# Output weights loaded head by head, border values stored through SyncE: a two-block transformer on one core

## Chip, cores and metric

One Trainium2 chip, one of its cores. The metric is the device time of one execution in microseconds (us); the kernel before takes 3176.66 us (median of three runs, 3176.52 to 3177.76). The engines are TensorE (PE, with its weight loads as PEld), VectorE (DVE), ScalarE (ACT), GpSimd (POOL) and SyncE (SP, which here only issues DMAs).

## The reference

Four blocks, A, B, A, B, each added to its input after a layer norm. A is a recurrent attention over segments of 32 tokens: 8 memory rows and the segment's 32 rows attend to each other in 32 heads of width 192, and the first 8 rows of the result are the memory of the next segment. B is a linear attention. Cut to A and the order of the blocks:

```python
for s in range(n_seg):                       # 64 segments, one after the other
    h = concatenate([mem, x[:, 32*s:32*s+32]])
    q, k, v = h @ Wq, h @ Wk, h @ Wv         # 640 -> 32 heads x 192
    p = softmax(mask(q @ k.T * 192**-0.5))
    o = einsum('bhte,hed->btd', p @ v, Wo)   # 32 x 192 -> 640
    mem = o[:, :8]; outs.append(o[:, 8:])
x = x + A(layernorm(x)); x = x + B(layernorm(x))
x = x + A(layernorm(x)); x = x + B(layernorm(x))
```

## The kernel before

Each A layer has two stages. **The batched stage** (`A_pre`) works out what doesn't depend on the recurrence: for the last 8 tokens of every segment (the border), keys and queries for all 64 segments in eight passes `keys_and_queries(h, r)`. Here h is a half (32 segments) and r a round, a group of 8 heads. One pass is 120 products of 128x256, evicted in turn by DVE and ACT into a staging buffer (`sts`, two of them) and stored to DRAM as `kqb` with one DMA of 1536 KB. Passes go in pairs (two halves of one round). Beside them `first_values(r)` works out border values of the first segments, evicts them into buffers `vts` and stores each to DRAM (`vb`, 97 KB, two blocks of 64 rows of 776 bytes) with `store_values`, through POOL. In layer 0 the same stage also normalises all rows: small steps of that are run one after each eviction, and POOL issues their loads (`ln_x`) and stores (`xn`).

**The chain** (`A_chain`) then runs the 64 segments, each in four rounds, forward in even segments and backward in odd ones. A round projects Q, K and V (20 products of 128x384 each), takes scores (L1191), attends, and multiplies by the output weights (`wo_round`, L1263). POOL loads the border keys and queries (`load_kqb`, L1123) and values (`extra_v`, L1134) and copies them in (L1130) ahead of the scores. Segment s+1 begins with the memory that segment s gives, so a segment that is late makes all that follow late.

**Output weights.** SBUF holds most weights; some stream in again in every segment. A round's output weights are 12 pieces of 640 columns (128 partitions, 164 KB). Rounds 1 and 2 lie whole in `wo_mid`, the first four pieces of rounds 0 and 3 in `wo_own`, and their other eight share `wo_both` and are streamed in turn (`load_both`, L797, four DMAs of two pieces). The matrix in the input has its rows in another order than the kernel's partitions. So layer 0 first copies all four rounds into a DRAM tensor `wo_rows` in the right order (`lay_out_wo`, L816, 32 DMAs of 240 KB), and `load_wo` (L774) takes from there two pieces at a time over all 128 partitions. `early_wo` and `late_wo` are the places of these loads: part in the batched stage, part in segment 0 of the chain. The staging buffers and the buffers of the border values lie where output weights will lie, so those loads wait for the stores out of them.

**What sets the order.** In layer 0's batched stage and in the chains every engine runs in the order of the code. In layer 2's batched stage only SP does, and a scheduler places the others. SP issues its DMAs strictly in order: one that waits holds up all behind it. SP and ACT issue to one set of eight completion counters that the program hands out in turn; a DMA waits until the one eight places earlier has landed. POOL has eight of its own. `load_slot` (L748) refills the slots of streamed Q, K and V weights; in the chain it is tied to the PE step that frees the slot.

**Constants.** `factors` gives four small tables for masks, which POOL builds in `build_A_consts`. They lie in the tensor `under`, where the chain later keeps its output row.

Of the kernel before, what the change touches and what calls it, by code (L numbers as in the profile page):

```python
# [8 lines left out]
P = 128  # L9
BF16 = mybir.dt.bfloat16  # L10
# [8 lines left out]
OWN = 4  # L19
# [4 lines left out]
VH = 194  # L24
# [98 lines left out]
class Kernel:  # L123
# [139 lines left out]
    def kept_tokens(self, k):  # L263
        return (self.later_tokens if k else self.under[:, self.ot_at:self.ot_at + 320]).rearrange("p (b t) -> p b t", b=self.KC)

    def first_rows(self):
        return self.under[:, self.ot_at + 576:self.ot_at + 736]
# [425 lines left out]
    def factors(self):  # L693

        at, out = self.ot_at + 2 * VH + 384, []
        for n in (64, 64, 16, 16):
            out.append(self.under[:, at:at + n])
            at += n
        return out

    def layer_A(self, xn_dram, at_dram, li, x_raw=None):
        nc, tc = self.nc, self.tc
# [9 lines left out]
        wov = self.A_Wo.rearrange("h d m -> (h d) m").rearrange("(q j f) m -> q f j m", j=6, f=32)  # L712
# [50 lines left out]
        early = {(2, 4), (2, 5), (1, 0), (1, 1), (1, 2), (1, 3), (0, 0), (0, 1), (0, 4), (0, 5)}  # L763

        def load_wo(r, part):
            for k in part:
                if r in (0, 3):
                    for i in (2 * k, 2 * k + 1):
                        assert (i < OWN) == (2 * k < OWN)
                    into = wo_own[r][:, 1280 * k:1280 * k + 1280] if 2 * k < OWN else \  # L770
                        wo_both[:, 1280 * k - own:1280 * k + 1280 - own]
                else:
                    into = wo_mid[:, 7680 * (r - 1) + 1280 * k:7680 * (r - 1) + 1280 * k + 1280]
                nc.sync.dma_start(out=into, in_=self.wo_rows[r, :, 1280 * k:1280 * k + 1280])  # L774
# [21 lines left out]
        def load_piece(into, r, c):  # L796
            self.last_load = nc.sync.dma_start(out=into[:, c:c + 1280], in_=self.wo_rows[r, :, own + c:own + c + 1280])  # L797
            return self.last_load
# [10 lines left out]
        if li == 0:  # L809
            self.wo_rows = dram.tile([4, P, 7680], BF16, name="wo_rows")  # L810

        def lay_out_wo(rs):
            for r in rs:
                for h in range(4):
                    for G in range(2):
                        nc.sync.dma_start(out=self.wo_rows[r, 32 * h:32 * h + 32, 3840 * G:3840 * G + 3840]  # L816
                                          .rearrange("f (j m) -> f j m", m=640), in_=wov[8 * r + 4 * G + h])

        def early_wo(first):
            sooner = {(0, 0), (0, 1), (2, 4), (2, 5)}  # L820
            for r in (0, 2, 1):
                load_wo(r, [k for k in range(6) if (r, k) in early and ((r, k) in sooner) == first])

        def late_wo(r, part=range(6)):
            load_wo(r, [k for k in part if (r, k) not in early])
# [10 lines left out]
    def A_pre(self, xn_dram, li, load_matrix, piece, wo_mid, wo_end, lay_out_wo, early_wo, x_raw):  # L836
# [10 lines left out]
        sts = [wo_mid[:, 6144 * i:6144 * i + 192 * SH].rearrange("p (s f) -> p s f", f=192) for i in range(2)]  # L847
        vts = [wo_end[:, 2 * VH * i:2 * VH * i + 2 * VH] for i in range(2 * NR + 1)]
        self.later_tokens = wo_end[:, (4 * NR + 2) * VH:(4 * NR + 2) * VH + 320]
        with ExitStack() as es:  # L850
# [6 lines left out]
            xT = [wo_end[:, 5120 - 1280 * i:6400 - 1280 * i] for i in range(2)]  # L857
            xB = None
            if x_raw is None:
                xB = [[self.view(LATE - 1280 * (i + 1), 1280) for i in range(2)],  # L860
                      [wo_mid[:, 12288 + 640 * i:12288 + 640 * i + 640] for i in range(2)]]
                xT[0] = self.next_xT[:, :]
# [71 lines left out]
            def first_values(r):  # L934
                for k, G in ((0, 0), (0, 1), (1, 0))[0:2 if r else 3]:
                    ps = ps_.tile([P, 512], F32, name="ps_pre", tag="bank")
                    self.tail_values(ps, lambda b: self.kept_tokens(k)[:, b, :], r, G, piece)
                    vt = vts[2 * NR if k else 2 * r + G]
# [3 lines left out]
            nc.vector.memset(wo_end[:, 0:(4 * NR + 2) * VH], 1.0)  # L942
            if x_raw is not None:
                first = [norm_tasks(lambda x, k=k: gather(x, x_raw, 0, k, (nc.sync, nc.scalar)),
                                    lambda xn, k=k: normed.__setitem__((0, k), xn)) for k in range(NT)]
                for step in zip(*first):
                    for f in step:
                        f()
                warm = ps_.tile([P, 512], F32, name="ps_warm", tag="bank")

                def busy(n):
                    for _ in range(n):
                        nc.tensor.matmul(warm[:, :], lhsT=self.ident[:, :], rhs=wo_end[:, 0:512],
                                         start=True, stop=True, skip_group_check=True)

                busy(12)
# [46 lines left out]
            if x_raw is not None:  # L1003
# [22 lines left out]
                keys_and_queries(0, 0)  # L1026
                first_values(0)
                keys_and_queries(1, 0)
                early_wo(False)
            else:  # L1030
# [4 lines left out]
                first_values(0)  # L1035
                self.build_A_consts()
# [6 lines left out]
                early_wo(True)  # L1043
                keys_and_queries(1, 2)
                first_values(2)
                keys_and_queries(0, 3)
                keys_and_queries(1, 3)
                first_values(3)
                load_round(0)
                keys_and_queries(0, 1)  # L1050
                first_values(1)
                keys_and_queries(1, 1)
                early_wo(False)
# [4 lines left out]
    def A_chain(self, xn_dram, at_dram, li, load_slot, piece, late_wo, load_both, wo, low):  # L1058
# [3 lines left out]
        with tc.tile_pool(name=f"A{li}_ch", reuse_waits="tile", bufs=1) as sp, \  # L1062
# [261 lines left out]
            late_wo(0)  # L1324
# [5 lines left out]
            for s in range(NSEG):  # L1330
# [26 lines left out]
                if s == 0:  # L1357
                    late_wo(3, range(OWN // 2))
# [27 lines left out]
                for n in range(L):  # L1386
# [164 lines left out]
```

## Time and profile before

| | |
|---|---|
| median of three runs | 3176.66 us |
| the profiled execution | 3169.9 us |
| its span | 3168.0 us |
| PE busy | 95% of the span |
| DMA, mean over the span | 237 GB/s |
| vb stores through POOL, layer 0 | 9, landing in 6.0 to 11.9 us |
| copies into `wo_rows` | 32 of 240 KB, landing in 8.1 us |
| loads from `wo_rows` | 560 of 320 KB, landing in 4.8 us |

The profile is of one execution. A row of a timeline has the start, the length, the engine, the line, the instruction and its tiles, a count, and in brackets the idle time before it with what ended it. "issue" means that the engine waited for nothing that the profile shows. A row of DMA queues has packets, MB and the share of sixteen DMA engines that they took in the stretch: q1 is SP's queue, q10 ACT's, q0 POOL's.

### The profile page before, as it was taken

The numbers are of one execution on the slowest core, as the hardware profiler recorded it, in microseconds if no ns is written. First come the engines' busy times: TensorE is split into PE (matmuls) and PEld (weight loads), VectorE is DVE, ScalarE is ACT, GpSimd is POOL, SyncE is SP. The second block draws the span as 40 slices with busy tenths as digits, with TensorE's granted clock in tenths as the row PEclk, the third lists the DMA queues.
The fourth block names the chain that finished last, engine by engine and source line by source line (L and its number), as shares of the span: only waits on it lengthen the run. The fifth ranks groups of instructions, "written<-read, shape, count | busy, mean of one in ns | idle before, by whom it ended". The sixth has DMA issues, their size and how long they took to land.

```text
span 3168.0 us, 141538 instructions
## 1 busy us (share of the span) xinstructions
PE 2993.8 (95%) x59586; PEld 1920.6 (61%) x59586; DVE 2184.4 (69%) x5426; ACT 1906.3 (60%) x4536; POOL 1392.8 (44%) x2872
## 2 busy tenths in 40 slices
PE   8789999999999999899999999999999999998999
PEld 7656666666666665555377566666666666665553
DVE  5467777777777777656644677777777777776565
ACT  3356666666666666646433566666666666666453
POOL 3255555555555555430122555555555555554300
PEclk9999999999999999999999999999999999999999
DMA  9977777877877877840268777777877777778300
GB/s 377 340 263 257 261 248 251 265 257 250 272 252 251 267 256 246 288 166 1 103 246 320 257 255 246 263 264 245 264 259 249 255 261 255 246 259 287 130 1 34
DMA packets 338873, 749.67 MB, mean 237 GB/s; under 512 B 68874, under 2 KB 115330, under 8 KB 335166
## 3 DMA queue, kind: packets, MB, share of 16 engines
q1 hardware_dynamic: 267998, 636.89, 58.3%
q0 software_dynamic: 69376, 100.10, 10.9%
q8 instruction: 469, 7.68, 1.0%
q10 hardware_dynamic: 864, 3.64, 0.3%
q14 instruction: 166, 1.36, 0.1%
HBM read 670.77 MB, written 78.01 MB: 236 GB/s over the span
## 4 chain that ended last, share of the span: by engine, by line
PE 76%; DVE 8%; DMA 6%; issue 5%; ACT 3%; POOL 2%; ACTq 0%; DVEq 0%; SPq 0%; POOLq 0%
PE ps_qk_k L1154 13%; PE ps_qk_q L1154 13%; PE ps_v L1154 12%; PE ps_w L1263 11%; PE ps_s L1191 6%; PE ps_pre L985 4%; PE ps_o L1204 3%; PE kv L1506 2%; DVE raws L1453 2%; ACT raws L1234 2%; DVE hT L1455 2%; PE ps_pq L517 2%; PE ps_t L1217 1%; PE ps_wo L466 1%; DVE QK L1377 1%
## 5 line engine op out<-in xcount | busy, mean ns | idle before, releaser
L1154 PEld LDWEIGHTS <-hT 128*32 128x32 bf16 x30720 | 787.1, 96 | 461.0 <-DVE hT L1455 78.7
L1174 DVE STREAM_TRANSPOSE QK<-raws 128x512 bf16<-128x512 bf16 (+1 forms) x1152 | 730.0, 642 | 219.3 <-ACT raws L1169 163.7
L1130 POOL COPY QK<-kqb 64x192 bf16<-64x192 bf16 x1024 | 349.5, 341 | 486.6 <-PE ps_s L1191 254.1
L1154 PE MATMUL ps_qk_q<-arena,hT 128*32 128x384 bf16 x10240 | 511.3, 327 | 41.4 <-DVE hT L1455 25.6
L1154 PE MATMUL ps_qk_k<-arena,hT 128*32 128x384 bf16 x10240 | 510.1, 328 | 3.0 <-ACT E L1273 1.4
L1169 ACT ACTIVATE raws<-ps_qk_k 128x512 bf16<-128x512 f32 (+1 forms) x640 | 313.5, 510 | 254.0 <-PE ps_qk_k L1154 243.5
L1234 ACT ACTIVATE raws<-ps_o,under 128x192 bf16<-128x192 f32 x1024 | 373.8, 420 | 121.9 <-DVE under L1228 102.5
L1154 PE MATMUL ps_v<-arena,hT 128*32 128x384 bf16 x8192 | 428.4, 326 | 4.0 <-issue 3.0
L1169 ACT ACTIVATE raws<-ps_qk_q 128x512 bf16<-128x512 f32 x512 | 305.7, 597 | 166.6 <-PE ps_qk_q L1154 153.1
L1134 POOL DMA_DIRECT2D Vp<-vb x512 | 257.9, 504 | 316.6 <-PE ps_t L1217 210.7
L1123 POOL DMA_DIRECT2D kqb<-kqb x512 | 292.4, 571 | 69.7 <-POOL QK L1130 59.4
L1191 PEld LDWEIGHTS <-QK 128*80 128x80 bf16 x4096 | 196.0, 121 | 184.9 <-issue 153.8
L1183 DVE CAST Vp<-ps_v 64x384 bf16<-64x384 f32 x512 | 286.3, 559 | 24.5 <-ACT Vp L1181 8.7
L1263 PE MATMUL ps_w<-arena,under 128*32 128x320 bf16 x6144 | 280.6, 300 | 9.5 <-DMA arena<-wo_rows 4.1
L1191 PE MATMUL ps_s<-QK 128*80 128x80 bf16 x4096 | 253.4, 209 | 21.8 <-POOL QK L1130 13.6
L1181 ACT ACTIVATE Vp<-ps_v 64x384 bf16<-64x384 f32 x512 | 246.4, 481 | 35.1 <-PE ps_v L1154 33.6
L1273 ACT ACTIVATE E<-ps_s 80x320 bf16<-80x320 f32 x512 | 217.7, 425 | 42.8 <-PE ps_t L1217 28.6
L985 PEld LDWEIGHTS <-arena 128*128 128x128 bf16 x1920 | 187.9, 98 | 31.0 <-issue 4.7
L1119 POOL DMA_DIRECT2D attn<-under x128 | 91.3, 713 | 262.0 <-DVE under L1115 223.5
L1112 ACT ACTIVATE raws<-ps_w 64x160 f32<-64x160 f32 x256 | 76.6, 299 | 201.1 <-DVE raws L1453 199.6
L1204 PE MATMUL ps_o<-Vp,E 80*32 80x193 bf16 x4096 | 180.3, 248 | 10.2 <-issue 5.7
L1263 PEld LDWEIGHTS <-under 128*32 128x32 bf16 x6144 | 147.2, 96 | 41.6 <-issue 9.8
(167 smaller groups left out, 4360.5 us busy)
## 6 DMA issues: line engine op xcount, KB each, us to landing
arena<-wo_rows SPq DMA_DIRECT2D x560, 320.0 KB, 4.8
arena<-in_A_Wq_dram SPq DMA_DIRECT2D x427, 384.0 KB, 4.5
arena<-in_A_Wk_dram SPq DMA_DIRECT2D x298, 384.0 KB, 5.6
arena<-in_A_Wv_dram SPq DMA_DIRECT2D x290, 384.0 KB, 5.9
kqb<-kqb POOLq DMA_DIRECT2D x512, 48.0 KB, 4.3
kqb<-arena POOLq DMA_DIRECT2D x14, 1536.0 KB, 9.7
Vp<-vb POOLq DMA_DIRECT2D x512, 24.2 KB, 3.8
otb<-otb POOLq DMA_DIRECT2D x256, 48.0 KB, 4.0
```

Of the source, the lines that this page charges most:

```text
L985: nc.tensor.matmul(ps[:, T * i:T * i + T], lhsT=w[b][:, P * c:P * c + P], rhs=xBT[:, b, :], start=(b == 0), stop=(b == KC - 1))
L1123: nc.gpsimd.dma_start(out=kqb[:], in_=self.kqb_d[r, :, s, :])
L1130: nc.gpsimd.tensor_copy(out=o, in_=kqb[h, :].rearrange("p (x c q) -> p x c q", c=3, q=16))
L1134: nc.gpsimd.dma_start(out=Vs[n % 2][64:80, :], in_=self.vb_d[s // 8, r].rearrange("g (t s) x f -> s (g t) (x f)", s=8)[s % 8])
L1154: last = nc.tensor.matmul(o, lhsT=hT[:, b, :], rhs=rhs, start=(i == 0), stop=(i == KC - 1), tile_position=(0, 32 * g), skip_group_check=True)
L1169: nc.scalar.activation(out=raw[:, c], in_=ps[:, c], func=ACT.Copy)
L1174: nc.vector.transpose(out=o, in_=i)
L1183: nc.vector.tensor_copy(out=o, in_=i)
L1191: nc.tensor.matmul(S[0:80, c0:c0 + 80], lhsT=KT[:, 4 * x + c, :], rhs=QT[:, 4 * x + c, :], start=(c % 2 == 0), stop=(c % 2 == 1), skip_gro ...
L1204: nc.tensor.matmul(O[G][32 * h:32 * h + 32, VH * G:VH * G + 193], lhsT=E[0:80, 80 * h + 32 * G:80 * h + 32 * G + 32], rhs=V[0:80, VH * h:V ...
L1234: nc.scalar.activation(out=out, in_=i, func=ACT.Copy, scale=rc[G])
L1263: step = nc.tensor.matmul(W[q:q + 32, 0:320], lhsT=OT[i // 6][:, i % 6 // 2, 32 * (i % 2):32 * (i % 2) + 32], rhs=rhs, start=(first and i ...
```

## The change

- `lay_out_wo` copies only the streamed pieces (4 to 11) of rounds 0 and 3, in 16 DMAs. `wo_rows` shrinks from four rounds of 7680 columns to two of 5120.
- `load_wo` takes a range of pieces and loads it straight from the input, in four DMAs of 32 partitions (one for each head of a group, `h`), 1280 bytes at a stretch. Every other load of output weights but the streamed ones goes this way, in both layers.
- `first_values` no longer stores. It puts its buffers on a list, and `store_made` stores them through SP, at places written into SP's order: after the rounds' values, among weight loads.
- In layer 0 the values of rounds 1 and 0 move one pass ahead each, from after pass (1, 1) to before it, and from after (0, 0) to before it. In layer 2 those of round 1 move ahead of pass (0, 1).
- The staging moves: `sts` from 0 and 6144 to 0 and 9216 in `wo_mid`; border values in six places of `wo_end`, the first three of which are used twice; the two memsets there are shorter (2 x 1280 columns for 3492); the turned rows `xT` and `xB` move, the second set of kept tokens goes to `under`, and the mask tables move 28 columns up.
- The places of the loads change: more in the batched stage (26 of 40 pieces in both layers), and in segment 0 of the chain (2, 2..11) in round step 1 and (3, 0..3) in step 2.

```diff
         def load_wo(r, i0, i1):
             G = i0 // 6
+            assert i1 <= 6 * G + 6 and (i1 <= OWN or i0 >= OWN or r in (1, 2))
+            if r in (1, 2):
+                into = wo_mid[:, 7680 * (r - 1) + 640 * i0:7680 * (r - 1) + 640 * i1]
+            else:
+                into = wo_own[r][:, 640 * i0:640 * i1] if i1 <= OWN else wo_both[:, 640 * i0 - own:640 * i1 - own]
+            for h in range(4):
+                nc.sync.dma_start(out=into[32 * h:32 * h + 32, :].rearrange("f (j m) -> f j m", m=640),
+                                  in_=wov[r, G, h, :, i0 - 6 * G:i1 - 6 * G])
...
-            self.wo_rows = dram.tile([4, P, 7680], BF16, name="wo_rows")
+            self.wo_rows = dram.tile([2, P, both], BF16, name="wo_rows")
+        def lay_out_wo():
+            for r in (0, 3):
                 for h in range(4):
+                    for G, i in ((0, OWN), (1, 6)):
+                        n = 640 * (6 * G + 6 - i)
+                        nc.sync.dma_start(out=self.wo_rows[r // 3, 32 * h:32 * h + 32, 640 * (i - OWN):640 * (i - OWN) + n]
+                                          .rearrange("f (j m) -> f j m", m=640), in_=wov[r, G, h, :, i - 6 * G:6])
...
-        sts = [wo_mid[:, 6144 * i:6144 * i + 192 * SH].rearrange("p (s f) -> p s f", f=192) for i in range(2)]
-        vts = [wo_end[:, 2 * VH * i:2 * VH * i + 2 * VH] for i in range(2 * NR + 1)]
+        sts = [wo_mid[:, 9216 * i:9216 * i + 192 * SH].rearrange("p (s f) -> p s f", f=192) for i in range(2)]
+        vt_at = [c + 2 * VH * i for c in (3840, 3840, 1280) for i in range(3)]
...
-                    self.store_values(nc.gpsimd, vt, k, r, G)
+                    made.append((vt, k, r, G))
+            def store_made():
+                while made:
+                    self.store_values(nc.sync, *made.pop(0))
...
                 load_round(1)
+                store_made()
                 load_round(0)
                 fetch_first_rows()
-                lay_out_wo((0, 2, 1))
-                early_wo(True)
-                lay_out_wo([3])
                 keys_and_queries(0, 2)
                 keys_and_queries(1, 2)
                 first_values(2)
+                store_made()
+                early_wo([(0, 0, 4), (0, 8, 12), (1, 10, 12), (2, 0, 2)])
+                lay_out_wo()
                 keys_and_queries(0, 1)
+                first_values(1)
                 keys_and_queries(1, 1)
-                first_values(1)
+                first_values(0)
+                store_made()
                 keys_and_queries(0, 0)
-                first_values(0)
                 keys_and_queries(1, 0)
-                early_wo(False)
+                early_wo([(0, 6, 8), (0, 4, 6), (1, 0, 6), (1, 6, 10)])
...
-            late_wo(0)
...
-                if s == 0:
-                    late_wo(3, range(OWN // 2))
...
+                    if s == 0 and n == 1:
+                        late_wo([(2, 2, 6), (2, 6, 12)])
...
-                    if s == 0 and n == 1:
-                        late_wo(1)
-                        late_wo(2)
+                    if s == 0 and n == L - 1:
+                        late_wo([(3, 0, 4)])
```

`store_made()` in the first line above stands after `first_values(3)`. In layer 2 it follows the values of rounds 0, 2 and (for 3 and 1 together) 1, with `early_wo([(0, 0, 4), (0, 4, 6), (0, 8, 12), (1, 10, 12), (2, 0, 2)])` after the loads of rounds 3 and 1 and `early_wo([(0, 6, 8), (1, 0, 6), (1, 6, 10)])` at the end. A triple is a round, its first piece and the piece after its last.

More of the change, by code (lines that the diff above doesn't have):

```diff
@@ L693, in factors @@
     def factors(self):
-        at, out = self.ot_at + 2 * VH + 384, []
+        at, out = self.ot_at + 800, []
         for n in (64, 64, 16, 16):
@@ L762, in layer_A, with load_wo @@
                 wo[r, i] = wo_own[r][:, 640 * i:640 * i + 640] if i < OWN else wo_both[:, 640 * (i - OWN):640 * (i - OWN + 1)]
[L763 to L774, printed above, removed]
+        def load_wo(r, i0, i1):
+            G = i0 // 6
+            assert i1 <= 6 * G + 6 and (i1 <= OWN or i0 >= OWN or r in (1, 2))
[6 more added lines that the diff above has]
+                                  in_=wov[r, G, h, :, i0 - 6 * G:i1 - 6 * G])
         held = []
@@ L796, in load_piece @@
         def load_piece(into, r, c):
-            self.last_load = nc.sync.dma_start(out=into[:, c:c + 1280], in_=self.wo_rows[r, :, own + c:own + c + 1280])
+            self.last_load = nc.sync.dma_start(out=into[:, c:c + 1280], in_=self.wo_rows[r // 3, :, c:c + 1280])
             return self.last_load
@@ L856, in A_pre @@
                 es.enter_context(tc.manual_schedule(engines={nc.sync.engine}))
-            xT = [wo_end[:, 5120 - 1280 * i:6400 - 1280 * i] for i in range(2)]
+            xT = [wo_end[:, 2560 - 2560 * i:3840 - 2560 * i] for i in range(2)]
             xB = None
```

44 lines of the change are left out of this document (22 added, 22 removed).

## Prediction

> **What bounds the kernel now.** I read the page first (busy shares and the chain), then a table of ten-microsecond stretches over the first 250 us and around 1,700 us, and there the timelines of TensorE (PE), GpSimd (POOL), SyncE (SP) and ScalarE (ACT), and SP's own waits.
>
> ```profile
> PE 2993.8 (95%) x59586; PEld 1920.6 (61%) x59586; DVE 2184.4 (69%) x5426; ACT 1906.3 (60%) x4536; POOL 1392.8 (44%) x2872
> ...
> PE 76%; DVE 8%; DMA 6%; issue 5%; ACT 3%; POOL 2%; ACTq 0%; DVEq 0%; SPq 0%; POOLq 0%
> ```
>
> PE sets the pace almost everywhere, and the change takes no work from it. So only a stretch where PE stands idle can pay. The diff touches the batched stages of the two A layers and the first segment of each chain. These are the stretches (columns: length, then busy PE, PEld, DVE, ACT, POOL, granted clock, DMA share, GB/s):
>
> ```profile
> 130.00:140.00 10.00, 5.73 (x100) 3.61 (x97) 5.25 (x13) 3.02 (x5) 0.81 (x1) 1.00 0.61 226
> 140.00:150.00 10.00, 0.00 (x0) 0.00 (x0) 0.00 (x0) 0.00 (x0) 2.96 (x5) 0.55 0.96 295
> 160.00:170.00 10.00, 5.42 (x116) 3.41 (x116) 4.00 (x11) 3.11 (x8) 2.96 (x7) 1.00 1.04 386
> ```
>
> PE runs until the batched stage ends near 132 and then stands empty or starved. The PE timeline, with the chain's next segment starts:
>
> ```profile
> 118.84 13.27 PE L985 MATMUL ps_pre<-arena 128*128 128x256 bf16 x120
> 136.51 0.99 PE L1154 MATMUL ps_qk_q<-arena,hT 128*32 128x384 bf16 x20
> 150.95 1.09 PE L1191 MATMUL ps_s<-QK 128*80 128x80 bf16 x8 [13.45 <-POOL QK L1130]
> 173.42 0.99 PE L1263 MATMUL ps_w<-arena,raws 128*32 128x320 bf16 x12 [0.60 <-DMA arena<-wo_rows]
> 177.67 1.37 PE L1154 MATMUL ps_qk_q<-arena,hT 128*32 128x384 bf16 x20
> ...
> 196.33 1.00 PE ps_qk_q L1154 x20
> ```
>
> Call T the end of the last batched product, 118.84 + 13.27 = 132.1. Segment 1 starts at 177.67, that is T + 45.6. A normal segment is 196.33 - 177.67 = 18.7 us, so about 25 us are lost in segment 0: one wait of 13.45 us on POOL, and the rest mostly on late loads. POOL's timeline tells the first:
>
> ```profile
> 127.09 0.81 POOL L261 DMA_DIRECT2D vb<-arena  x1 [4.72 <-DVE arena L94]
> 135.07 0.81 POOL L261 DMA_DIRECT2D vb<-arena  x1 [7.17 <-issue]
> 142.60 0.80 POOL L261 DMA_DIRECT2D vb<-arena  x1 [6.72 <-issue]
> 143.39 1.18 POOL L1123 DMA_DIRECT2D kqb<-kqb  x2
> 150.56 0.74 POOL L1130 COPY QK<-kqb 64x192 bf16<-64x192 bf16 x2 [5.00 <-DMA kqb<-kqb]
> ```
>
> The border-value stores (vb) block POOL 7 us each, and the chain's first loads (kqb) stand behind them. SP and ACT tell the second:
>
> ```profile
> 133.01 0.35 ACTq L994 DMA_DIRECT2D kqb<-arena  x1
> 138.83 1.20 SPq L816 DMA_DIRECT2D wo_rows<-in_A_Wo_dram  x2
> 142.81 8.06 SPq L774 DMA_DIRECT2D arena<-wo_rows  x8
> ...
> SPq L816 <- DMA kqb<-arena: 12.1, 1, 12.1
> ```
>
> In the built program SP's and ACT's DMAs share eight completion counters in turn, so SP waited 12.1 us for ACT's last kqb store (issued 133.01, landed 138.83: 5.8 us). Only at 142.8 could the output weights start.
>
> **The change part by part.** *vb stores from POOL to SP.* POOL's nine stalls go; its loads of rows are no longer late for DVE. Three PE waits of the batched stage hang on that:
>
> ```profile
> 70.93 1.82 PE L257 MATMUL ps_pre<-arena,under 128*64 128x384 bf16 x20 [2.61 <-DVE arena L94]
> 100.37 0.35 PE L257 MATMUL ps_pre<-arena,under 128*64 128x384 bf16 x2 [1.32 <-DVE arena L94]
> 111.82 4.53 PE L985 MATMUL ps_pre<-arena 128*128 128x256 bf16 x40 [0.80 <-DVE arena L94]
> ```
>
> I take all three, -4.7 us; if POOL's row loads are late anyway, 0. The shorter first memset (2560 columns for 3492) gives up to 0.6. In the new order the kqb store of pass (0,0) goes out 12 us before T, so the first scores, due at T + 5.4 (137.5 now), find their kqb: the 13.45 us go. If the r=0 border values land late, the next to wait is the first attention product.
>
> On SP nine vb stores now stand in the row with the weights. What each costs:
>
> ```profile
> q0 software_dynamic: 192, 0.10, 8.1%
> ...
> DMA to landing us min/median/max: 6.0/7.6/11.9
> ```
>
> The first row is a 6 us stretch with one store alone (1634 to 1640): 8.1% x 16 x 6 = 7.8 engine-us for 97 KB. It lands in 6.0, so it runs on about two engines, 3.9 us on each. Two at 57 us and two at 85 us stand in front of weights with 15 to 20 us to spare, so they are hidden there. But the r=1 values now reuse the buffer of the first r=2 store (issued about 85, landing 7.6 later, at 93), while their eviction is due at 85. ACT waits, and PE has seven more banks of 1.1 us each (ten of 120 products in 13.27 us), to 92.3. I take a new PE wait of 2 us, 0 to 8. Then T = 132.1 - 0.6 - 4.7 + 2 = 128.8 (126.8 to 134).
>
> The last five stores are 19.5 us on their two engines, from about 113 if the shorter copy ends there; they end just before the gate below. Costed at nothing, up to +5.
>
> *Only two matrices' streamed parts copied.* 16 copies (2.6 MB) for 32 (7.9 MB). The copies lie under full PE, so their gain is only SP time.
>
> *Head-by-head loads.* Four DMAs of 32 partitions for one of 128, in 1280-byte runs. Rows for their rate, each a queue's packets, MB and share of 16 engines in a stretch:
>
> ```profile
> q1 hardware_dynamic: 5445, 14.87, 77.9%
> q1 hardware_dynamic: 4986, 6.71, 57.8%
> q1 hardware_dynamic: 1472, 2.67, 87.0%
> q10 hardware_dynamic: 192, 0.16, 10.8%
> q10 hardware_dynamic: 144, 1.57, 16.4%
> q0 software_dynamic: 434, 0.50, 6.6%
> ```
>
> The first (10 to 60 us) is weights: 14.87 MB in 0.779 x 16 x 50 engine-us, 382 GB/s. The second (86 to 118) is the copies, 1280-byte reads: 363. The third (143 to 152) is mostly loads from the copied rows: 341. The fourth (0 to 6) is 32-partition rows of 1280 bytes into SBUF: 246. The last two (1724 to 1750) are ACT's kqb store, 4.3 us, and POOL's small loads, 1.7. The new loads lie between 246 and 363. The fourth row is nearest but made of 40 KB pieces, so I take 280.
>
> The Trainium skill, page "SBUF — State Buffer", section "Door 1: The DMA port swizzle", speaks against this edit: a transfer to 32 or 64 partitions of one half reaches 8 of 16 SBUF ports, about 218 GB/s at best. The row of 246 is above that, so the trace agrees only in that it is the slowest of the four; at 218 the sum below would be some 7 us worse.
>
> *Where the loads stand.* SP is gated once more: the fourth quarter of (1,0,6) is eight counters behind ACT's kqb store, so SP goes on at T + 0.9 + 5.8 = T + 6.7. Behind it are 19.5 pieces of 164 KB of output weights (3.19 MB; before, 32 pieces, 5.24 MB), seven slot weights (2.75 MB), four streamed pieces (1.31 MB): 11.4 + 7.2 + 3.8, plus 2 of small loads, 24.4 us (21.8 to 26). The same sum for before, 15.4 + 7.2 + 3.8 + 2 = 28.4, against 30.6 from 142.8 to 173.42, leaves 2.2 for landing. From the last late piece to segment 1 it was 4.25. So segment 1 starts at T + 6.7 + 24.4 + 2.2 + 4.3 = T + 37.6 = 166.4: -11.3 us. PE alone would allow T + 20.4; the loads hide that.
>
> *The constants.* The small factors no longer overlap the output row, and six POOL instructions of layer 2 (about 1.2 us) now run in layer 0's segment 0, while POOL would wait for PE. Nothing; 1.2 if that cover is gone.
>
> *Layer 2:*
>
> ```profile
> 1710.45 13.27 PE L985 MATMUL ps_pre<-arena 128*128 128x256 bf16 x120
> 1724.30 1.00 PE L1154 MATMUL ps_qk_q<-arena,hT 128*32 128x384 bf16 x20 [0.58 <-DVE ps_qk_q L1090]
> 1738.37 0.51 PE L1154 MATMUL ps_qk_q<-arena,hT 128*32 128x384 bf16 x4 [2.92 <-DMA arena<-in_A_Wq_dram]
> 1750.23 0.99 PE L1263 MATMUL ps_w<-arena,raws 128*32 128x320 bf16 x12 [0.36 <-DMA arena<-wo_rows]
> 1754.49 1.44 PE L1154 MATMUL ps_qk_q<-arena,hT 128*32 128x384 bf16 x20
> ```
>
> Here POOL held nothing; segment 0 takes 30.2 us, bound by loads. The third Q slot now stands behind ACT's kqb store, so the 2.92 stays. Pieces still to load near T are 24 against about 24. At 280 for 341 GB/s they cost 2.5 more, and they may start some 4 us earlier (after the kqb store of (0,1), not behind vb). I take -1 (-5 to +3).
>
> Sum: -11.3 - 1 = -12.3 on the profiled execution's 3169.9 us (span 3168.0). The median of the runs shown, 3176.66, lies 6.8 above that, so the forecast is 3164.4.
>
> **The rivals.** *More gain:* the strips run like the copies (363) and the r=2 store lands in time: T = 126.8, segment 1 at T + 35.0 = 161.8, -15.9, layer 2 -4.7: 3156. For it: the 363 row; against: the 246 row.
>
> *Half rate for strips:* a transfer to 32 partitions is fed at half the 341 GB/s of one to 128 (170). Then 3.19 MB cost 18.8 (+7.4) and layer 2's 3.93 MB 23.1 (+9.1): 3181. For it: 246 is below 341; against: it isn't half. This is the skill page's rule above as it would act here; by the page's own 218 GB/s the time would be about 3172.
>
> *The other side: POOL's spacing moves to SP.* If SP too can't issue past one vb store until it has drained (7 to 11.5 us on POOL; take 9), the five stores from 113 hold SP to 158, segment 1 starts at 158 + 30.9 = 189 (+11), and four stores in layer 2 hold its loads from 1697 to 1733, 9 late: 3197. It decides from 7 us a store (SP free at 148). For it: nothing shows two such stores in a row on SP; against: in the chain SP issues one every segment in 0.5 us and goes on.
>
> *Next to nothing:* the eviction wait puts T at 134 and SP comes to its gate 4 us late: segment 1 at 134 + 4 + 37.6 = 175.6, -2.1, so 3174 with layer 2's -1 lost in it.
>
> **How the numbers follow.** Forecast 0.57 (own range 3158 to 3170), more gain 0.16, half rate 0.14, SP's spacing 0.08, next to nothing 0.05. From no change a measurement of this kernel can tell about 0.2%, 6.4 us: faster is the first two, same the third and fifth, slower the fourth. Range 3153 to 3175: it takes in more gain and the late T of 134, and leaves out SP's spacing and the half rate.
>
> **What would show it.** Right: no POOL wait of PE near 137; T near 129; a PE wait on an eviction near 93; SP standing still until ACT's kqb store lands; PE waits on Q, K, V slots and output weights in segment 0; segment 1 near 166; layer 2's segment 1 within 5 us of 1754 less the shift. Wrong: T at 132 or later, segment 1 before 158, direct loads under 200 GB/s, several microseconds between vb issues on SP, or any difference in segments 2 to 62, which I cost at nothing.

## The result, and the profile after

The changed kernel takes 3197.12 us (median of nine runs) against 3176.52 of the kernel before on the same chip. The ratio is 1.0066, 95% interval 1.0047 to 1.0085: 20.6 us slower, where 12.3 us faster was forecast and the whole range lay below the kernel before. In the two profiled executions the spans are 3197.7 and 3168.0, 29.7 apart. One kernel below, before_vb_sp_spread, left only the trace of an execution at a granted clock of 0.61, which is not read here.

The page of the changed kernel, busy times and the chain that ended last:

```profile
PE 3001.9 (94%) x59552; PEld 1923.1 (60%) x59586; DVE 2185.1 (68%) x5428; ACT 1909.8 (60%) x4536; POOL 1381.9 (43%) x2854
...
PE 75%; DMA 10%; DVE 7%; issue 3%; ACT 2%; POOL 2%; SPq 1%; ACTq 0%; DVEq 0%; POOLq 0%
```

The DMA share of that chain went from 6 to 10%: more of it is waiting for transfers. PE's timeline in layer 0 (T is again the end of the last batched product):

```profile
105.45 7.76 PE L992 MATMUL ps_pre<-arena 128*128 128x256 bf16 x50 [13.40 <-ACT arena L96]
115.71 26.38 PE L992 MATMUL ps_pre<-arena 128*128 128x256 bf16 x240
147.41 0.50 PE L1203 MATMUL ps_s<-QK 128*80 128x80 bf16 x8
163.94 0.51 PE L1166 MATMUL ps_qk_q<-arena,hT 128*32 128x384 bf16 x4 [5.79 <-DMA arena<-in_A_Wq_dram]
179.69 0.99 PE L1275 MATMUL ps_w<-arena,raws 128*32 128x320 bf16 x12 [4.65 <-DMA arena<-in_A_Wo_dram]
189.69 1.79 PE L1166 MATMUL ps_qk_q<-arena,hT 128*32 128x384 bf16 x20
```

The three waits on DVE and the 13.45 us on POOL ahead of the first scores are gone, as forecast. In their place PE stands 13.40 us for one eviction (ACT itself stood 21.56 us until an earlier store out of the same buffer had landed), T is 115.71 + 26.38 = 142.1 (128.8 forecast, 132.1 before), and segment 1 starts at 189.69 (166.4 forecast, 177.67 before): 12.0 us lost. Layer 2:

```profile
1723.68 13.26 PE L992 MATMUL ps_pre<-arena 128*128 128x256 bf16 x120
1755.63 0.51 PE L1166 MATMUL ps_qk_q<-arena,hT 128*32 128x384 bf16 x4 [5.24 <-DMA arena<-in_A_Wq_dram]
1772.08 0.99 PE L1275 MATMUL ps_w<-arena,raws 128*32 128x320 bf16 x12 [5.32 <-DMA arena<-in_A_Wo_dram]
1780.74 0.99 PE L1275 MATMUL ps_w<-arena,QK 128*32 128x320 bf16 x12 [3.17 <-DMA arena<-in_A_Wo_dram]
1783.40 1.79 PE L1166 MATMUL ps_qk_q<-arena,hT 128*32 128x384 bf16 x20
```

The last batched product ends at 1736.9 (1723.7 before, 13.2 later, about the loss of layer 0), segment 1 starts at 1783.40 (1754.49 before): segment 0 takes 46.5 us for 30.8, another 15.7. So 27.7 of the 29.7 us lie in the two segments 0 and what stands ahead of layer 0's. SP's timeline shows what they waited for (start, length of the group in SP's order, what is loaded or stored, count):

```profile
94.97 0.60 SPq L1008 DMA_DIRECT2D under<-xn  x1
96.09 2.80 SPq L261 DMA_DIRECT2D vb<-arena  x2
98.94 13.72 SPq L773 DMA_DIRECT2D arena<-in_A_Wo_dram  x16
112.70 14.42 SPq L817 DMA_DIRECT2D wo_rows<-in_A_Wo_dram  x16
127.22 11.09 SPq L261 DMA_DIRECT2D vb<-arena  x5
138.43 18.22 SPq L773 DMA_DIRECT2D arena<-in_A_Wo_dram  x16
...
1690.70 17.07 SPq L773 DMA_DIRECT2D arena<-in_A_Wo_dram  x20
...
1720.21 12.15 SPq L261 DMA_DIRECT2D vb<-arena  x4
1732.46 14.25 SPq L773 DMA_DIRECT2D arena<-in_A_Wo_dram  x12
```

SP has no gap of over 0.6 us between 95 and 156 us. Before, the first rows (`under<-xn`) were issued at 81.44, now at 94.97; the first r=2 store follows at 96, where 85 was assumed. The five stores take 11.1 us of SP's order, the four of layer 2 take 12.2, each ahead of loads for which PE then waits. The values were ready: the last was evicted at 118.8, the first of the five stores went out at 127.22.

### The profile page after: what moved, and what is told of

It reads as the page before. It is cut to its first block, busy times and chain, and to the rows that moved or that the text cites. A ratio compares the mean times of both kernels' runs of the same rounds, so it can differ in the third digit from the quotient of the medians.

```text
span 3197.7 us, 141552 instructions
## 1 busy us (share of the span) xinstructions
PE 3001.9 (94%) x59552; PEld 1923.1 (60%) x59586; DVE 2185.1 (68%) x5428; ACT 1909.8 (60%) x4536; POOL 1381.9 (43%) x2854
## 4 chain that ended last, share of the span: by engine, by line
PE 75%; DMA 10%; DVE 7%; issue 3%; ACT 2%; POOL 2%; SPq 1%; ACTq 0%; DVEq 0%; POOLq 0%
PE ps_qk_k L1166 13%; PE ps_qk_q L1166 12%; PE ps_v L1166 12%; PE ps_w L1275 10%; PE ps_s L1203 6%; PE ps_pre L992 6%; PE ps_o L1216 2%; PE kv L1516 2%; DMA arena<-in_A_Wo_dram 2%; DVE raws L1463 2%; DMA arena<-wo_rows 2%; DVE hT L1465 2%; PE ps_pq L518 1%; ACT raws L1246 1%; DMA arena<-in_A_Wv_dram 1%
## 5 line engine op out<-in xcount | busy, mean ns | idle before, releaser
L1195 DVE CAST Vp<-ps_v 64x384 bf16<-64x384 f32 x512 | 286.2, 559 | 27.9 <-ACT Vp L1193 12.3
L1131 POOL DMA_DIRECT2D attn<-under x128 | 91.5, 714 | 274.3 <-DVE under L1127 239.6
L992 PE MATMUL ps_pre<-arena 128*128 128x256 bf16 x1440 | 161.3, 275 | 15.9 <-ACT arena L96 15.0
```

Source lines behind the costliest of these rows:

```text
L992: nc.tensor.matmul(ps[:, T * i:T * i + T], lhsT=w[b][:, P * c:P * c + P], rhs=xBT[:, b, :], start=(b == 0), stop=(b == KC - 1))
L1195: nc.vector.tensor_copy(out=o, in_=i)
```

## The experiments

Two theories. **V**: the price is the border-value store itself. Its outer dimension is 2, two DMA engines carry it, and whatever queue it stands in is held. **S**: the price is the loads by strips of 32 partitions. (The first expectation has a third, **O**: the new order is bad whoever stores.) All results, each with the kernel before measured on the same chip; one tenth of a per cent is 3.2 us:

| run | kernel | ratio to before | 95% |
|---|---|---|---|
| (the change) | stores whole, on SP | 1.0066 | 1.0047 to 1.0085 |
| vb_pool | changed, stores whole, on POOL | 1.0097 | 1.0079 to 1.0115 |
| vb_spread | changed, stores split, on SP | 0.9996 | 0.9980 to 1.0011 |
| pool_spread | changed, stores split, on POOL | 0.9976 | 0.9960 to 0.9993 |
| vb_buf | changed, other buffers for round 1 | 1.0095 | 1.0080 to 1.0110 |
| vb_buf2 | the same, one load moved | 1.0080 | 1.0055 to 1.0104 |
| before_vb_sp | before, stores whole, on SP | 1.0040 | 1.0025 to 1.0056 |
| before_vb_sp_spread | before, stores split, on SP | 0.9973 | 0.9958 to 0.9989 |
| before_vb_pool_spread | before, stores split, on POOL | 0.9947 | 0.9928 to 0.9965 |
| strips_only | before, loads by strips | 1.0031 | 1.0016 to 1.0045 |
| strips_pool_spread | the same, stores split, on POOL | 0.9959 | 0.9940 to 0.9979 |
| spread_rest | vb_spread, layer 2 without strips | 0.9994 | 0.9981 to 1.0008 |
| pool_spread_rest | pool_spread, layer 2 without strips | 0.9969 | 0.9955 to 0.9984 |
| rest_in_B | the same, copies in the first B layer | 0.9942 | 0.9926 to 0.9959 |
| before_pool_spread_kqb | before_vb_pool_spread, last kqb store on POOL | 0.9925 | 0.9906 to 0.9944 |
| rest_in_B_kqb | rest_in_B, last kqb store on POOL | 0.9943 | 0.9925 to 0.9961 |

**Whose queue: vb_pool.**

```diff
-                    self.store_values(nc.sync, *made.pop(0))
+                    self.store_values(nc.gpsimd, *made.pop(0))
```

> The changed kernel with one edit: the border-value stores (vb) go through POOL again, at the same places of the program. Theory V (the nine stores in SP's order hold SP, and through the reused buffer PE): the 13.4 us wait for the eviction and the late loads of layer 2 (17 us) go, POOL's spacing of some 7 us a store comes back, and its last five stores (from about 104 us) may hold the chain's first kqb loads as before: 3197 - 13 - 17 + 5 to 10 = 3172 to 3180. Theory S (the loads from the input in strips of 32 partitions are what is slow): only the 13.4 us go, layer 2 stays as late as it is: 3184 to 3190. Theory O (what was moved lies badly: more loads behind the last gates, whoever stores vb): 3190 or more.

1.0097, no better than on SP, so the first two expectations are missed and the time falls in O's range. PE's timeline: POOL's stall is back.

```profile
149.95 1.09 PE L1203 MATMUL ps_s<-QK 128*80 128x80 bf16 x8 [12.91 <-POOL QK L1142]
```

SP, without one border-value store in its order, took 24.20 us for the 16 strips of 124.30: for 16.3 of them it waited for one kqb store to land, which POOL had issued only at 136.82, behind the border-value stores. Taking the stores out of SP's order does not help by itself; V as I had worded it (stores in *SP's* order) falls.

**The shape: vb_spread.**

```diff
-        queue.dma_start(out=self.vb_d[k, r, G].rearrange("c x f -> x c f"), in_=vt)
+        for x in range(2):
+            queue.dma_start(out=self.vb_d[k, r, G, :, x], in_=vt[64 * x:64 * x + 64, :])
```

> The changed kernel with one edit: each border-value store becomes two DMAs of 64 partitions by 776 bytes, so that the outer dimension of a DMA is 64 and not 2. Theory V, if the price lies in a store that only two DMA engines carry: a store lands in 2 to 4 us and not 6.6, SP issues the five stores of layer 0 in under 6 us (11.1 now) and layer 2's four in under 6 (12.2 now); PE's eviction wait falls by 2 to 4 us: 3197 - 5 - 6 - 3 = 3183, 3178 to 3190. If the price is the full queue in front of the stores (SP stands behind weight loads whatever the shape), or under theory S: 3194 to 3200.

(The chain's own border stores come from the same function and are split too.) 0.9996: all of the 20.6 us are gone, a little more than V asked for. The rows of the last stores of layer 0 on SP (count, then min/median/max in ns of SP's time for one), first the changed kernel, then this one:

```profile
L261 SPq DMA_DIRECT2D vb<-arena x5: 537/1914/5412, 127.2 to 132.9; - x5
L262 SPq DMA_DIRECT2D vb<-arena x10: 498/598/1584, 119.9 to 128.1; - x10
```

The 6.6 us of the expectation is not the landing of a store: it is that of POOL's loads `Vp<-vb`, which are rows of the same tile. For whole stores on SP the trace has no landing, so whether the halves land sooner than they isn't shown. SP's and PE's timelines of this run:

```profile
86.83 0.67 SPq L1009 DMA_DIRECT2D under<-xn  x1
...
119.88 9.02 SPq L262 DMA_DIRECT2D vb<-arena  x10
128.94 17.55 SPq L774 DMA_DIRECT2D arena<-in_A_Wo_dram  x16
...
1701.38 8.61 SPq L262 DMA_DIRECT2D vb<-arena  x8
```

```profile
99.04 8.09 PE L993 MATMUL ps_pre<-arena 128*128 128x256 bf16 x50 [6.47 <-ACT arena L96]
178.80 1.81 PE L257 MATMUL ps_x<-arena,tT 128*64 128x384 bf16 x10
...
1760.42 1.81 PE L257 MATMUL ps_x<-arena,tT 128*64 128x384 bf16 x10
```

The first rows go out 8.1 us earlier than in the changed kernel, the strips behind the last stores 9.5 earlier (128.94 for 138.43), segment 1 begins at 178.80 + 1.81 = 180.6, 9.1 earlier. Twice as many stores take less of SP's order (9.0 for 11.1 us, 8.6 for 12.2), but 7.3 of those 9.5 us were there before the last stores of layer 0 (119.88 for 127.22). How the whole stores ahead of them lose those 7.3 us isn't resolved by the rows. Part is chance: in the two kernels of the next test, whose stores are whole too, the first rows went out at 91.5 and 91.4, not at 94.97. PE's eviction wait halves.

**Is PE's 13.4 us wait the price? vb_buf, vb_buf2.**

```diff
-        vt_at = [c + 2 * VH * i for c in (3840, 3840, 1280) for i in range(3)]
+        vt_at = [3840, 4228, 4616, 1280, 3840, 4228, 1668, 2056, 4616]
```

> The changed kernel with one edit: the border values of round 1 in layer 0 take the buffers of round 3, stored some 35 us before, and no longer those of round 2. Stores stay on SP. Theory V: PE's wait of 13.4 us at 92 us goes, the last batched product ends near 128.7 where it ended at 142.1, but the output weights' loads behind the stores then wait on SP rather than on PE, so only part of it reaches segment 1: 4 to 13 us, and layer 2 is as before: 3184 to 3193. Theory S: the loads in strips set segment 1 alone (they start after the five stores on SP, and these after the copies): no more than 5 us, 3192 to 3197.

1.0095, outside both expectations. The edit brought a wait of its own: the last of the five stores now leaves from where pieces (0, 6..7) are loaded, so the 16 strips began at 150.03 for 138.43. vb_buf2 moves that load to the end of its group:

```diff
-                early_wo([(0, 6, 8), (0, 4, 6), (1, 0, 6), (1, 6, 10)])
+                early_wo([(0, 4, 6), (1, 0, 6), (1, 6, 10), (0, 6, 8)])
```

> The changed kernel, stores unsplit on SP, with the values of round 1 of layer 0 in the buffers of round 3, and the load of the pieces (0, 6..7), which waits for the last of the five stores, moved to the end of its group. If PE's 13.4 us eviction wait set the end of layer 0's batched stage and that the rest: segment 1 comes 8 to 13 us earlier than 189.7, 3183 to 3190. If SP's order binds (loads, stores, copies and strips one after another, 59 to 180 us without a pause) and PE's wait lay beside it: segment 1 within 4 us of 189.7, POOL or slots waiting in its place, 3192 to 3202.

1.0080, not told apart from the change itself. PE's timeline:

```profile
104.45 26.37 PE L992 MATMUL ps_pre<-arena 128*128 128x256 bf16 x240
148.64 1.09 PE L1203 MATMUL ps_s<-QK 128*80 128x80 bf16 x8 [7.63 <-POOL QK L1142]
...
188.03 1.81 PE L257 MATMUL ps_x<-arena,tT 128*64 128x384 bf16 x10
```

T is 130.8, as forecast within 2 us, and segment 1 still begins at 189.8 (189.7 in the changed kernel). SP's strips began at 138.09, as before the edit. The largest wait of PE in that stage was worth nothing: SP's order set the end, and PE waited at one place or at another (for POOL at the first scores, then for pieces).

**The parts alone on the kernel before.** before_vb_sp moves only the stores (`nc.sync` for `nc.gpsimd`), before_vb_sp_spread splits them as well, before_vb_pool_spread splits them on POOL, with the edit of vb_spread.

> The kernel before with one part of the change alone: its border-value stores go through SP instead of POOL, one DMA each as before, where each value is evicted. Theory V (the two-engine store is the price): POOL's 13.45 us stall at the first scores goes, but SP's loads come later by some 2 to 5 us for each of the last five stores in layer 0 and of the stores in layer 2: 3174 to 3190. If only the reused buffers and the new places of the loads made the stores dear: 3160 to 3168.

> The kernel before with the stores through SP and each of them split in two DMAs of 64 partitions. Theory V: the stall of 13.45 us goes and SP is held little; the late loads (T + 6.7 + 28.4 + 2.2 + 4.3 by the terms of the prediction, T near 128) then put segment 1 near 169.6, 8 us ahead of 177.7: 3162 to 3169. If layer 0's loads on SP bind whatever POOL does: 3172 to 3178.

> The kernel before with the stores left on POOL, each split in two DMAs of 64 partitions. If POOL's 7 us behind each store come from the two engines that carry it: the gaps fall to some 2 us, the 13.45 us stall to under 4, and the three PE waits of 4.7 us go: 3162 to 3170. If POOL pays per DMA whatever its shape: 18 DMAs for 9, the stall grows: 3180 to 3195.

Moving alone costs 0.40% (12.7 us), as V had it, but at another place than expected: the last seven stores stand behind the copies in SP's order, and POOL, which waits for the values, comes later still. Segment 1 of layer 0 begins 18.0 us later than before; layer 2's segment 0 is no longer than before. SP and PE of before_vb_sp:

```profile
147.53 12.71 SPq L261 DMA_DIRECT2D vb<-arena  x7
...
167.41 1.09 PE L1191 MATMUL ps_s<-QK 128*80 128x80 bf16 x8 [28.01 <-POOL QK L1130]
```

Split, the same move gains 0.27%, as expected. Split on POOL, with nothing moved, the gain is 0.53% (17 us), more than expected (3151.33 us). POOL's timeline and PE's there:

```profile
99.64 2.14 POOL L262 DMA_DIRECT2D vb<-arena  x4
...
114.91 2.63 POOL L262 DMA_DIRECT2D vb<-arena  x5 [0.19 <-issue]
...
153.16 0.46 PE L1264 MATMUL ps_w<-arena,under 128*32 128x320 bf16 x4 [13.83 <-DMA arena<-wo_rows]
```

The 7 us behind each store are gone (0.5 us a half), and so is the stall at the scores; PE runs until its next wait, for pieces out of the copies, and segment 1 begins only 2.4 us earlier than before.

So with whole stores on SP, split on SP, whole on POOL and split on POOL the kernel before stands at 1.0040, 0.9973, 1 and 0.9947, the changed one at 1.0066, 0.9996, 1.0097 and 0.9976. Splitting gains 0.5 to 1.2% in each of the four pairs. At equal stores the changed kernel is 0.2 to 0.3% behind (1.0% with whole stores on POOL). pool_spread had been expected at 3163 to 3170 us if the shape is the price on either queue, and took 3162.62.

These pairs do not price the batched stage's stores alone: the chains' own stores, 110 in the two chains and through SP in every kernel, are split with them. By the starts of the segments in PE's timelines, 14.3 of the 23.0 us between the profiled executions of the changed kernel and vb_spread lie in the two segments 0 and ahead of layer 0's, and 6.9 in the segments behind them; of the 18.3 us between the kernel before and before_vb_pool_spread only 4.2 and as much as 16.7. From segment 1 to 63 the seven traces with whole stores take 1141.6 us on average in layer 0 and 1141.4 in layer 2; with split stores it is 1138.1 and 1137.1 (seven and nine traces, those with copies in layer 0's chain left out of the first), with ranges that overlap. So perhaps 8 us of what splitting gains comes from the chains. No run splits the stores of one stage alone.

**The strips: strips_only, strips_pool_spread.** The kernel before with `load_wo` in four DMAs of 32 partitions and 16 copies for 32:

```diff
-                nc.sync.dma_start(out=into, in_=self.wo_rows[r, :, 1280 * k:1280 * k + 1280])
+                for h in range(4):
+                    nc.sync.dma_start(out=into[32 * h:32 * h + 32, :].rearrange("f (j m) -> f j m", m=640),
+                                      in_=wov[8 * r + 4 * G + h, :, i0 - 6 * G:i1 - 6 * G])
```

> The kernel before with one part of the change alone: output weights that are not streamed are loaded head by head from the input (four DMAs of 32 partitions for one of 128, neighbouring pieces together), and only the streamed parts are copied (16 copies for 32). Stores, order and buffers are those of before. Theory V: strips are near neutral: 16 copies fewer on SP against loads at 250 to 300 GB/s for 341, 3165 to 3180. Theory S: layer 2 loses its 9 to 17 us and layer 0 some, 3185 to 3200.

> The kernel before with split stores on POOL (3151 as measured) and the loads by strips, copies only of the streamed parts. Theory S: the strips cost the 8 us that they cost alone, 3156 to 3163. If fewer copies on SP pay once POOL holds nothing (PE waited 13.83 us there for pieces out of the copies): 3140 to 3150.

Alone they cost 0.31% (10 us, between the two expectations); with split stores 0.12%, which its interval does not tell from nothing. In strips_only layer 0's segment 1 begins as before (177.7), layer 2's some 6 us later, with a segment 0 of 37.9 us for 30.8; the longest wait there:

```profile
1750.55 0.72 PE L1272 MATMUL ps_w<-arena,under 128*32 128x320 bf16 x8 [5.59 <-DMA arena<-in_A_Wo_dram]
```

**Layer 2 without strips: spread_rest, pool_spread_rest, rest_in_B.** The parts that aren't streamed are copied too, after layer 0, into a second tensor, and layer 2 loads them over 128 partitions:

```diff
+            if li:
+                nc.sync.dma_start(out=into, in_=self.wo_rest[r, :, 640 * i0:640 * i1] if r in (1, 2) or i1 <= OWN
+                                  else self.wo_rows[r // 3, :, 640 * i0 - own:640 * i1 - own])
+                return
```

> The changed kernel with the split stores (3176 as measured) and one more edit: the parts of the output weights that are not streamed are copied as well, after layer 0 in the first B layer, where the trace shows the DMA engines idle (shares 0.00 to 0.15 from 1420 to 1520 us), and layer 2 loads them over 128 partitions, one DMA for four. Theory S for layer 2: its segment 0 (41.4 us from the last batched product to segment 1 with split stores, 30.9 before) falls to 31 to 35: 3166 to 3170. If not the strips but the number and place of the late loads are what costs there: 3174 to 3179.

> The same, and layer 2's output weights over 128 partitions from copies made in the first B layer, now tied to a step of that layer so that none lies among the chain's loads. The two findings together: layer 2's segment 0 took 29.1 us with such loads for 41.4 with strips, so some 8 to 12 us less than the kernel with split stores on POOL: 3152 to 3160, about 15 us under the kernel before. If the two gains are one and the same wait: 3163 to 3170.

Both ratios stayed where they were (the 3169 us of spread_rest lie in the first range only because the kernel before was lower in that set too), though segment 0 of layer 2 fell to 29.0 and 28.9 us, as expected. The rows of the new tensor in pool_spread_rest (its writes) say why:

```profile
L826 SPq DMA_DIRECT2D wo_rest<-in_A_Wo_dram x24: 551/594/1057, 165.8 to 262.5; - x24
```

The scheduler had put the copies into the first segments of layer 0's chain, where weights stream: its first ten segments took 190.3 us for 186.0. My expectation that none would lie there was wrong, and some 4 us went there. rest_in_B puts a semaphore of the B layer ahead of each copy.

> The changed kernel with split stores on POOL (3162.6 as measured) and layer 2's output weights over 128 partitions, the copies for it now behind a semaphore of the first B layer, so that they run from about 1400 us, where the DMA engines are idle, and not in the chain's first segments (165 to 263 us in the two runs before, whose first ten segments took 190.3 and 191.3 us for 186.0 and 184.4 without copies). Theory S for layer 2: its segment 0 of 29 us for 37.6 now shows in the time: 3150 to 3157. If the strips of layer 2 are not what the changed kernel still loses: 3159 to 3166.

```profile
L825 SPq DMA_DIRECT2D wo_rest<-in_A_Wo_dram x24: 557/604/1365, 1406.2 to 1428.3; - x24
```

Now 0.9942 for 0.9976: 0.34%, 11 us, with intervals that just touch (the time itself, 3158.94, lies between the two expectations, as the kernel before was 5.7 us slower in that set). SP's and PE's timelines of layer 2 there:

```profile
1677.38 0.33 SPq L776 DMA_DIRECT2D arena<-wo_rest  x1
1678.02 1.23 SPq L776 DMA_DIRECT2D arena<-wo_rows  x2
1679.98 1.23 SPq L776 DMA_DIRECT2D arena<-wo_rest  x2
...
1709.35 13.26 PE L1013 MATMUL ps_pre<-arena 128*128 128x256 bf16 x120
1749.69 1.81 PE L257 MATMUL ps_x<-arena,tT 128*64 128x384 bf16 x10
```

The pieces for which the changed kernel issues 20 strips in 17.1 us go out in five loads within 3.8 us, and segment 0 takes 28.9 us (46.5 in the changed kernel, 37.6 in pool_spread). So without strips in layer 2 the changed order is level with the kernel before at equal stores (0.9947).

**The gate: before_pool_spread_kqb, rest_in_B_kqb.**

```diff
-                queue = nc.scalar if turn == NH * NR else nc.gpsimd
+                queue = nc.gpsimd
```

> The kernel before with split stores on POOL (3151.3 as measured) and its last kqb store on POOL too, not on ACT, so that SP's copies and loads stand behind no store of that engine. PE waited 13.83 us there for pieces loaded out of the copies. If that gate (SP stood at a copy until the store had landed) sets segment 1 of layer 0: 4 to 8 us less, 3143 to 3148. If the store's own landing and the staging buffers set it, not the counter: within 3 us, 3148 to 3154.

> Both together on the changed kernel: split stores on POOL, layer 2 over 128 partitions, last kqb store on POOL. SP waited about 10 us for ACT's store ahead of the Q slots in both layers (a slot load took 10.53 and 9.43 us to issue). If the gate costs: 4 to 8 us under the first kernel of this set, 3144 to 3152. If not: the same as that one within 3 us.

In the changed order the gate is worth nothing (0.9943 for 0.9942). In the old order segment 1 of layer 0 begins at 168.5 for 175.3, but the ratios (0.9925 and 0.9947) have intervals that overlap. This kernel, the old order with split stores on POOL and no kqb store on ACT, is the fastest tried by its ratio: 3153.57 us beside 3175.91 before. The 4 to 8 us expected show in that start, but not beyond the noise in the time.

## Why the prediction was wrong, step by step

- **The stores on SP, the step that failed.** "Two at 57 us and two at 85 us stand in front of weights with 15 to 20 us to spare, so they are hidden there", and the last five "costed at nothing, up to +5". They are not hidden. Moving them alone, with all else as before, costs 12.7 us (before_vb_sp), though it takes POOL's pauses away. In the changed kernel the five take 11.1 us of SP's order and layer 2's four 12.2, the five go out from 127 on where 113 was taken, and the 16 strips behind them begin at 138.4. There were no 15 to 20 us to spare: a slack read from the kernel before is not there in a queue that the change itself makes late. The prediction had the store's two engines and its 7.8 engine-us (its "lands in 6.0" is the least of layer 0; the store of that stretch landed in 5.0), and set these beside the gate, not the time that they take from an ordered queue. Splitting takes 22 us off the changed kernel, but 17 off the kernel before as well, and has a share in the chains: 22 is what the shape costs this kernel, not what the change lost by it.
- **SP's dates.** The first r=2 store was taken as "issued about 85", where the row of before has the first rows; it was issued at 96. From 50 to 80 us the queues carried (kernel before, then changed; q1 is SP's, q0 POOL's):

```profile
q1 hardware_dynamic: 2662, 7.28, 62.6%
q0 software_dynamic: 1169, 4.76, 39.4%
```

```profile
q0 software_dynamic: 1062, 6.49, 53.8%
q1 hardware_dynamic: 2180, 5.46, 46.9%
```

  Both times 12 MB in 30 us, with shares that add up to some 100%: the engines were full. POOL without its stalls moved 1.7 MB more, SP 1.8 MB less. It is so in sixteen traces: q1 has 6.8 to 7.3 MB in these 30 us where whole stores go through POOL (three kernels), 4.9 to 6.0 in the others. Of the 13.5 us by which the first rows came late some 5 are there without whole stores on SP (86.2 to 88.2 in vb_spread, vb_pool, pool_spread and before_vb_pool_spread), the others go with them (91.4 to 99.3 where whole stores stand on SP). That a freed POOL would take SP's bandwidth was not in the sum.
- **The eviction wait** was named, at its place and on its mechanism, at 2 us (0 to 8): 13.40, as the store that it waits for went out 11 us later than taken. But vb_buf2 shows that this size decided nothing.
- **The three PE waits and the 13.45 us** went as forecast; T without the eviction wait was 130.8 (128.8). The reason given for the 13.45 was half right: POOL's 7 us behind a store go with the store's shape, and splitting it removes them where they stood.
- **The strips.** Mis-sized were their rate, 280 GB/s, and with it their price in layer 2, 2.5 us with up to 4 given back. The strips travel in packets of 1280 bytes, by which the trace tells them from the other loads of SP's queue. In the changed kernel those of 99 to 112 us have 1.67 MB in 107.7 engine-us, 248 GB/s by the prediction's own reckoning (MB by engine time, times 16); from 1690 to 1707 it is 247, from 172 to 190 (segment 0) 192. In pool_spread all those from 1690 to 1757 have 4.71 MB in 355.0 engine-us: 212. The row that the prediction called nearest, 246, was the right one, or still too fast. At 212 layer 2's 3.93 MB take 7.0 us more than at 341, an estimate from these rates. Measured were 7.1 us of segment 0 (strips_only), 8.9 (strips_pool_spread) and 8.7 (pool_spread for rest_in_B), and 11 by the ratios of the last pair. SP's order may have a part in it, 20 DMAs for 5; rate and number were not told apart. The Trainium skill, page "SBUF — State Buffer", section "Door 1: The DMA port swizzle", gives some 218 GB/s for a transfer to 32 partitions. With 192 to 248 the traces agree better with that than with my 280.
- **The gate** at T + 6.7 did not bind: SP came to its last strips at 138.4 and left them at 156.7, 14.6 behind T, without having waited for a kqb store, and taking ACT's store away changed nothing in the new order.
- **The constants and segments 2 to 62**, costed at nothing: the first ten segments after segment 0 took 185.3 us for 186.2, and PE waited for no constant. Right.
- **The rivals.** "POOL's spacing moves to SP" gave 3197 with a chance of 0.08, and segment 1 of layer 0 at 189, as measured. The kernel is in its camp, but that the numbers agree is luck: SP spent 2.2 us on a store, not 9, below the 7 from which that rival decides, and was late before it came to the five stores. "More gain" falls. "Half rate" falls as worded (170 GB/s and 16.5 us, for 192 to 248 and some 10 us), though 212 lies nearer to 170 than to 280.

By the parts alone on the kernel before, the stores moved cost 12.7 us and the strips 10: 22.7 together, beside 20.6 measured. What is left for the order, the buffers and the places of the loads is some -2 us, not told from nothing. In the prediction the same two parts were a gain, the stall of 13.45 us gone, and a price of a few us.

## What to carry to other kernels

Before a small store is moved to another queue, read its outer dimension: splitting one of 2 into two of 64 was worth 0.5 to 1.2% in all four places here (some of it in the chains), and moving it whole cost 0.4%. In a stage where the DMA engines are full, freeing one queue takes bandwidth from the others, so dates on the other queues must be worked out anew and not read from the kernel before. The longest wait of an engine need not be the price: take it away and see whether the stage ends sooner.

## What the runs showed of the hardware

- A store of 97 KB with an outer dimension of 2 holds the engine that issues it. On SP, in before_vb_sp, the first of seven in a row took 0.5 us and each of the last four 2.3 to 2.4:

```profile
L261 SPq DMA_DIRECT2D vb<-arena x7: 528/2337/2437, 147.5 to 157.8; - x7
```

  On POOL, in layer 0 of the kernel before, nine such stores come with 46.3 us of "issue" (idle with nothing to wait for), their 18 halves in before_vb_pool_spread with 0.2. The halves do not land sooner there (8.9 to 11.2 us, the whole ones 6.0 to 11.9), but POOL goes on meanwhile, and they travel side by side. The Trainium skill, page "DMA: Bandwidth & Descriptors", section "Why a DMA increments its semaphore by 16 and not by 1", says how many engines carry a DMA: the largest number up to 16 that divides the slowest dimension of both sides. That gives 2 for a whole store and 16 for a half. The runs agree in that halves hold neither engine so, though no row shows the engines one by one; that POOL stands still behind such a DMA is told by these runs alone.
- Behind the waits of a segment 0 the products run slower for a while. Layer 2's segment 0 in the changed kernel and in the kernel before (length, busy PE, PEld, DVE, ACT, POOL, granted clock, DMA share, GB/s):

```profile
1737.00:1783.00 46.00, 23.08 (x426) 12.77 (x426) 14.12 (x39) 12.20 (x29) 10.67 (x23) 0.77 0.92 228
1724.00:1754.00 30.00, 22.34 (x424) 13.16 (x426) 13.87 (x37) 12.22 (x29) 10.69 (x23) 0.85 0.86 307
```

  The granted clock is 0.77 for 0.85, and 1.00 in both from 1800 to 1850 us. The first 20 products of segment 1 take 1.79 us in the changed kernel, 1.44 before, and 0.99 in the steady chain.
